# A fused linear-attention and feed-forward kernel: another form of the query feature map, an activation table taken early, one statistics pass moved

## The chip, the cores and the metric

The kernel runs on one core of a Trainium2 chip. The metric is the time of one execution on the device, in microseconds (us). A profile of one execution gives a span that is about 1.2 us shorter than the time of the same execution (209.1 of 210.31 for the kernel before). A run is called fast when it lies within 1.5% of the fastest run of its kernel; only fast runs are compared. All engines of the core are named as the profile names them: PE is the matmul engine (TensorE) and PEld its weight loads, DVE is VectorE, ACT is ScalarE, POOL is GpSimd, SP is the engine that issues most DMA transfers.

## The reference

One sequence of 2048 tokens of width 640 goes through a layer normalisation. Its result feeds a linear attention with 32 heads and a feed-forward block of width 1728, and the two are joined by a gate. Cut to what matters:

```python
xn = layernorm(x)
q, k, v = split(xn @ wqkv)                   # 32 heads of 20
phi = lambda t: where(t > 0, t + 1, exp(t)) + 1e-6
pq, pk = phi(q), phi(k)
kv  = einsum("bhsd,bhse->bhde", pk, v)
num = einsum("bhqd,bhde->bhqe", pq, kv)
den = einsum("bhqd,bhd->bhq", pq, sum_over_s(pk)) + 1e-6
s = (num / den) @ wo
u = relu(xn @ w1) @ w2
out = x + s * silu(u)
```

## The kernel before

The kernel works in this order: statistics, centring and transposes of the first four tiles of 128 tokens; keys; queries and `h = relu(xn w1)` by turns; the denominator of the attention; a Gram matrix of `xn` and the key features, from which `kv` follows; `kv` times `wo` as one fused weight; then `u` by 320-column products, the gates, and the output. Each `sc.op` puts one instruction on the named engine with the buffers that it reads (R) and writes (W).

The query feature map. A block of 128 features by 512 tokens stands in one of six PSUM banks; `er` holds three pairs of 16-bit buffers in SBUF:

```python
    def Q_block(j, f):
        b = nextb()                                   # a ring of 6 banks
        sc.group("PE", [... matmul(ps[b], lhsT=wq[:, k, ...], rhs=xnT[:, j, k, :]) for k in range(C)], ...)
        e_ = er[:, es, 0, :]
        r_ = er[:, es, 1, :]
        sc.op("ACT", lambda eng: eng.activation(out=e_, in_=ps[b], func=ACTF.Exp), ...)
        sc.op("DVE", lambda eng: eng.tensor_scalar(out=r_, in0=ps[b], scalar1=0.0, scalar2=1e-6,
                                                   op0=ALU.max, op1=ALU.add), ...)
        sc.op("DVE", lambda eng: eng.scalar_tensor_tensor(out=pqT[:, f, schunk(j)], in0=e_, scalar=1.0, in1=r_,
                                                          op0=ALU.min, op1=ALU.add), ...)
```

The head, where `bn` is the half-tile statistics pass (BATCH_NORM_STATS2) and `xcT_copy` takes transposed tiles out of PSUM:

```python
    K_mm(0, 2, 0, 1)
    transposes(1, 6)
    xcT_copy(0, 0, 1, "DVE")
    bn(0, 1)
    mean_act(2, 0)
    xcT_copy(1, 6, 0, "DVE")
    xcT_copy(1, 6, 1, "ACT")
    ...
    centre(2)
    transposes(2, 0)
```

The stretch where the fused weight meets the first gates. The reciprocal of the denominator goes through a scratch buffer in memory and comes back widened, in four parts, with which the query features are multiplied (`divide`):

```python
    load_recip(2)                        # DMA, issued by SP
    load_recip(3)
    fns = [...]                          # matmuls of the last Gram block
    lastG = sc.group("PE", fns, ...)
    sc.op("ACT", ... activation(out=GT[:, 4, :] ..., func=ACTF.Copy), ...)
    u_T(2); u_T(4)
    divide(1)
    ...
    def W_block(c, b):                   # one of six blocks of the fused weight
        sc.group("PE", ...)              # kv times wo: two matmuls
        # PSUM -> wtmp by VectorE (blocks 1 and 4) or ScalarE (the others), then row moves:
        dma("SP", lambda eng, q=q, e=e: eng.dma_start(wf[...], wtmp[...]), R=[("wtmp", c)], W=[("wf", q)])
    def gate_q(t, n, b):
        sc.op("ACT", lambda eng: eng.activation(out=g[:, HN*n:HN*(n+1)], in_=ps[b][:, 0:HN], func=ACTF.Silu), ...)
```

## Time and profile before

| | kernel before |
|---|---|
| time, median of 3 runs | 210.42 us (210.40 to 210.59) |
| profiled span | 209.1 us, granted PE clock 0.999 |
| busy: PE, VectorE, ScalarE, GpSimd | 204.3, 172.9, 109.1, 47.9 us |
| table load before the first gate | 1.28 us |
| PE standing before 138.65 us | 0.49 us |

The page of the kernel before: first the busy time of each engine with its share of the span and its instruction count, then the shares of the chain that ended last, then three of its groups (line, engine, operation, output and inputs, count; busy time and mean ns of one; idle time of the engine before them and what ended it).

```profile
PE 204.3 (98%) x1367; PEld 126.3 (60%) x1377; DVE 172.9 (83%) x321; ACT 109.1 (52%) x214; POOL 47.9 (23%) x71
...
PE 94%; ACT 2%; DVE 2%; DMA 1%; issue 0%
...
L580 DVE SCALAR_TENSOR_TENSOR pqT<-regE 128x512 bf16<-128x512 bf16 x20 | 17.0, 848 | 0.7
L578 DVE TENSOR_SCALAR regE<-psT 128x512 bf16<-128x512 f32 x20 | 13.6, 680 | 4.7 <-ACT regE L577 4.7
L577 ACT ACTIVATE regE<-psT 128x512 bf16<-128x512 f32 x20 | 11.9, 597 | 8.6 <-PE psT L570 8.1
```

The kernel is bound by PE. The two VectorE groups are the pair of passes that the change rewrites: 30.6 us of VectorE's 172.9, but their engine is not the one that ends last. There are 1377 weight loads and 1367 matmuls: ten matmul records are missing. Each missing record looks like a pause of 0.216 us between the starts of two PE instructions, and ten of the pauses that one could count in this trace are false.

The second pass has a wide spread. In the view of one line's instructions, the three figures after the colon are the shortest, median and longest in ns:

```profile
L580 DVE SCALAR_TENSOR_TENSOR pqT<-regE x20: 691/691/1816, 35.2 to 101.1; 128x512 bf16<-128x512 bf16 x20
```

The chain of waits in order of time (start, length, engine or cause), kernel before, its first part and the stretch before the first gate:

```profile
5.27 0.27 DVE regX L501
5.54 0.40 DVE stats L436
5.94 0.20 DVE regX L501
...
135.94 1.28 ACT L1043
137.22 0.01 issue
137.23 0.44 ACT wv_sb L1043
137.67 0.59 ACT reg L1017
138.26 0.34 ACT psT L806
138.60 0.05 issue
138.65 5.88 PE psT L799 x42
```

Most of the chain is PE itself. It leaves PE in the head, for a statistics pass that stands between two copies, and here, where ScalarE spends 1.28 us at L1043 with no operand. That is a table load for silu. The timeline of PE over the same stretch (start, length, then how many instructions; what the engine waited for stands in brackets) says what the load costs PE:

```profile
136.26 1.11 PE L799 MATMUL psT<-reg,regH 128*128 128x320 f16 x7
137.21 1.11 PE L799 MATMUL psT<-reg,regE 128*128 128x320 bf16 x7
138.65 0.58 PE L799 MATMUL psT<-reg,regH 128*128 128x320 f16 x3 [0.33 <-ACT psT L806]
```

Seven matmuls of 320 columns start 0.136 us apart: the group that began at 136.26 is followed by the next at 137.21, which is 0.95 us later. The group of 137.21 had thus given way at 138.16, and the next began at 138.65. PE lost 0.49 us of the 1.28 us that the load lasted; the queued matmuls covered the rest.

The timeline of VectorE, kernel before, at four places:

```profile
5.85 0.27 DVE L501 COPY regX<-psT 128x256 bf16<-128x256 bf16 x1
...
101.67 0.31 DVE L695 TENSOR_TENSOR zmat<-mh,psT 128x160 bf16<-128x160 f32 x1
...
130.43 1.56 DVE L737 TENSOR_TENSOR pqT<-pqT,reg 128x1024 bf16<-128x1024 bf16 x2 [1.24 <-DMA reg<-scr]
131.91 0.95 DVE L744 TENSOR_TENSOR reg<-psT,mv 128x360 bf16<-128x360 f32 x3
```

### The profile page before, as it was taken

What the parts mean: (1) busy time and instruction counts of PE and PEld (TensorE: products, weight loads), DVE (VectorE), ACT (ScalarE), POOL (GpSimd) and SP (SyncE); (2) the same over time, 40 slices, a digit from 0 to 9 for tenths busy, and PEclk for the clock granted to TensorE, in tenths of its full rate; (3) what the DMA queues carried; (4) which work ended last, traced back from release to release, by engine and by line L of the source; (5) the groups of instructions that cost most, each with busy time, mean ns of one, the idle gap of its engine ahead of it and who ended that gap; (6) DMA issues with size and microseconds to landing.
All of it is one profiled execution on the core that took longest, in us unless ns stands there. A gap on an engine that the chain in (4) does not pass through costs nothing.

```text
span 209.1 us, 3583 instructions
## 1 busy us (share of the span) xinstructions
PE 204.3 (98%) x1367; PEld 126.3 (60%) x1377; DVE 172.9 (83%) x321; ACT 109.1 (52%) x214; POOL 47.9 (23%) x71
## 2 busy tenths in 40 slices
PE   7999999999999999999999999999999999999995
PEld 7655554554554555444447777767777777777773
DVE  3988966798996899979997777888888989797465
ACT  5697766466665666655653432472435254343531
POOL 2278701111008389994000000000000000000001
PEclk9999999999999999999999999999999999999999
DMA  6988499122000217000189999337911010110103
GB/s 202 358 289 166 83 313 88 35 41 41 12 0 10 55 31 191 31 2 0 41 272 267 331 273 321 117 112 236 310 55 63 0 66 26 40 66 0 63 3 125
DMA packets 30359, 24.74 MB, mean 118 GB/s; under 512 B 12037, under 2 KB 30341, under 8 KB 30341
## 3 DMA queue, kind: packets, MB, share of 16 engines
q1 hardware_dynamic: 27013, 20.26, 35.0%
q10 hardware_dynamic: 3328, 4.24, 6.3%
q8 instruction: 11, 0.18, 0.4%
q14 instruction: 7, 0.06, 0.1%
HBM read 15.81 MB, written 5.24 MB: 101 GB/s over the span
## 4 chain that ended last, share of the span: by engine, by line
PE 94%; ACT 2%; DVE 2%; DMA 1%; issue 0%
PE psT L799 38%; PE psT L592 27%; PE psT L517 10%; PE psT L570 10%; PE psT L1218 3%; PE psT L1302 2%; DMA reg<-in_A_x_dram 1%; PE psT L611 1%; ACT reg L1017 1%; PE psT L983 1%; ACT L1043 1%; PE psT L704 1%; DVE stats L436 0%; PE psT L491 0%; PE psT L1009 0%
## 5 line engine op out<-in xcount | busy, mean ns | idle before, releaser
L592 PE MATMUL psT<-reg 128*128 128x512 bf16 x192 | 45.5, 379 | 0.3 <-issue 0.2
L596 ACT ACTIVATE regH<-psT 128x512 bf16<-128x512 f32 x52 | 30.8, 602 | 17.3 <-PE psT L592 17.3
L799 PE MATMUL psT<-reg,regH 128*128 128x320 bf16 (+1 forms) x224 | 34.4, 299 | 0.3 <-ACT psT L806 0.3
L592 PEld LDWEIGHTS psT<-reg 128*128 128x128 bf16 x195 | 18.9, 98 | 21.9 <-issue 0.4
L799 PEld LDWEIGHTS psT<-reg,regH 128*128 128x128 bf16 (+1 forms) x224 | 21.8, 98 | 9.1 <-ACT psT L806 0.7
L799 PE MATMUL psT<-reg 128*128 128x320 bf16 (+1 forms) x164 | 27.2, 299 | 0.0
L1211 POOL TENSOR_TENSOR reg<-reg 128x224 bf16<-128x224 bf16 x1 | 0.6, 605 | 109.5 <-DVE reg L1206 109.5
L528 POOL TENSOR_TENSOR wv_sb<-wv_sb,reg 128x640 f32<-128x640 f32 x16 | 24.0, 1501 | 1.9 <-DVE reg L552 1.0
L1043 ACT ACTIVATE wv_sb<-psT 128x320 bf16<-128x320 f32 x28 | 11.1, 437 | 25.2 <-PE psT L799 15.6
L744 DVE TENSOR_TENSOR psT<-psT,reg 128x320 f32<-128x320 f32 x30 | 14.3, 495 | 11.9 <-PE psT L799 11.1
L570 PE MATMUL psT<-reg 128*128 128x512 bf16 x95 | 23.8, 379 | 0.3
L534 ACT ACTIVATE regE<-psT 128x640 bf16<-128x640 f32 x24 | 15.6, 701 | 9.1 <-PE psT L517 9.1
L799 PEld LDWEIGHTS psT<-reg 128*128 128x128 f16 (+1 forms) x164 | 16.0, 98 | 6.4
L806 ACT ACTIVATE psT<-psT 128x320 f32<-128x320 f32 x32 | 13.7, 427 | 10.6 <-PE psT L799 10.0
L517 PE MATMUL psT<-reg 128*128 128x320 bf16 x120 | 18.3, 299 | 0.0
L580 DVE SCALAR_TENSOR_TENSOR pqT<-regE 128x512 bf16<-128x512 bf16 x20 | 17.0, 848 | 0.7
L578 DVE TENSOR_SCALAR regE<-psT 128x512 bf16<-128x512 f32 x20 | 13.6, 680 | 4.7 <-ACT regE L577 4.7
L570 PEld LDWEIGHTS psT<-reg 128*128 128x128 bf16 x100 | 9.8, 98 | 11.6
L806 ACT ACTIVATE reg<-psT 128x320 f32<-128x320 f32 (+1 forms) x22 | 9.6, 435 | 13.1 <-PE psT L799 13.1
L577 ACT ACTIVATE regE<-psT 128x512 bf16<-128x512 f32 x20 | 11.9, 597 | 8.6 <-PE psT L570 8.1
L436 DVE BATCH_NORM_STATS2 stats<-reg 128x6 f32<-128x320 bf16 x32 | 14.1, 474 | 2.3 <-DMA reg<-in_A_x_dram 2.3
L517 PEld LDWEIGHTS psT<-reg 128*128 128x128 bf16 x120 | 11.7, 98 | 6.5 <-DMA reg<-reg 0.2
(105 smaller groups left out, 305.2 us busy)
## 6 DMA issues: line engine op xcount, KB each, us to landing
scr<-rden SPq DMA_DIRECT2D x4, 640.0 KB, 10.0
reg<-in_A_x_dram SPq DMA_DIRECT2D x4, 640.0 KB, 6.1
out_dram<-reg SPq DMA_DIRECT2D x15, 160.0 KB, 1.9
reg<-in_A_x_dram SPq DMA_DIRECT2D x14, 160.0 KB, 3.4
reg<-scr SPq DMA_DIRECT2D x2, 640.0 KB, 7.4
regE<-scr SPq DMA_DIRECT2D x2, 640.0 KB, 7.2
reg<-in_B_w_dram ACTq DMA_DIRECT2D x1, 1040.0 KB, 7.1
reg<-in_A_wo_dram SPq DMA_DIRECT2D x6, 160.0 KB, 5.0
```

The lines of the kernel that those rows point to most:

```text
L436: sc.op("DVE", lambda eng: eng.bn_stats(stats[:, t, a, :], xv[:, HN * a:HN * (a + 1)]), R=[("xin", t % XR)], W=[("stats", t, a)])
L517: fns.append(lambda eng, a=a, k=k, lhs=lhs: eng.matmul(ps[b + a][:, 0:HN], lhsT=lhs, rhs=wk[:, k, HN * a:HN * (a + 1)], start=(k == 0), st ...
L528: sc.op("POOL", lambda eng: eng.tensor_tensor(out=zacc, in0=zacc, in1=pk[:, t, :], op=ALU.add), R=[("zacc",), ("pk", t)], W=[("zacc",)])
L534: sc.op("ACT", lambda eng: eng.activation(out=o_.rearrange("p (a n) -> p a n", a=2), in_=ps2(b, HN), func=func, scale=scale), R=[("ps", b) ...
L570: sc.group("PE", [(lambda eng, k=k: eng.matmul(ps[b], lhsT=wq[:, k, P * f:P * (f + 1)], rhs=xnT[:, j, k, :], start=(k == 0), stop=(k == C ...
L578: sc.op("DVE", lambda eng: eng.tensor_scalar(out=r_, in0=ps[b], scalar1=0.0, scalar2=1e-6, op0=ALU.max, op1=ALU.add), R=[("ps", b), ("er_e ...
L580: sc.op("DVE", lambda eng: eng.scalar_tensor_tensor(out=pqT[:, f, schunk(j)], in0=e_, scalar=1.0, in1=r_, op0=ALU.min, op1=ALU.add), R=[(" ...
L592: a = sc.group("PE", [(lambda eng, k=k: eng.matmul(ps[b], lhsT=w1_col(k, P * f, P), rhs=src[:, k, :], start=(k == 0), stop=(k == C - 1))) ...
L596: sc.op("ACT", lambda eng: eng.activation(out=hT[:, f, schunk(j)], in_=ps[b], func=ACTF.Relu), R=[("ps", b)], W=[("hT", j, f)])
L744: sc.op("DVE", lambda eng: eng.tensor_tensor(out=out, in0=in0, in1=in1, op=op), R=R, W=W, extra=extra)
L799: sc.group("PE", [(lambda eng, k=k, lhs=lhs, rhs=rhs: eng.matmul(ps[b][:, 0:HN], lhsT=lhs, rhs=rhs, start=(start and k == 0), stop=(k == n ...
L806: sc.op("ACT", lambda eng: eng.activation(out=dst, in_=ps[b][:, 0:HN], func=ACTF.Copy), R=[("ps", b)], W=[dkey], extra=extra)
```

## The change

It has three parts. First, the query feature map is written as max(x + 1, min(exp x, 1)). For x > 0 the first term is the larger, since x + 1 > 1; for x ≤ 0 the second is, since exp x ≥ x + 1. So one pass clips the exponential in place, in SBUF and in 16 bit, and a second pass reads PSUM and takes the maximum; the pass with two SBUF inputs is gone. Second, a one-column silu is put before the last Gram block, so that the table load falls into ScalarE's idle time there. Third, the statistics of tile 0's second half move behind the copy that they stood before.

```diff
@@ -573,13 +573,12 @@
         es = qi[0] % NER
         qi[0] += 1
         e_ = er[:, es, 0, :]
-        r_ = er[:, es, 1, :]
         sc.op("ACT", lambda eng: eng.activation(out=e_, in_=ps[b], func=ACTF.Exp), R=[("ps", b)], W=[("er_e", es)])
-        sc.op("DVE", lambda eng: eng.tensor_scalar(out=r_, in0=ps[b], scalar1=0.0, scalar2=1e-6, op0=ALU.max, op1=ALU.add),
-              R=[("ps", b), ("er_e", es)], W=[("er_r", es)])
-        sc.op("DVE", lambda eng: eng.scalar_tensor_tensor(out=pqT[:, f, schunk(j)], in0=e_, scalar=1.0, in1=r_,
-                                                          op0=ALU.min, op1=ALU.add),
-              R=[("er_e", es), ("er_r", es)], W=[("pqT", j, f)])
+        sc.op("DVE", lambda eng: eng.tensor_scalar(out=e_, in0=e_, scalar1=1.0, scalar2=1e-6, op0=ALU.min, op1=ALU.add),
+              R=[("er_e", es)], W=[("er_e", es)])
+        sc.op("DVE", lambda eng: eng.scalar_tensor_tensor(out=pqT[:, f, schunk(j)], in0=ps[b], scalar=1.0 + 1e-6,
+                                                          in1=e_, op0=ALU.add, op1=ALU.max),
+              R=[("ps", b), ("er_e", es)], W=[("pqT", j, f)])
 
     def hsrc(j):
         if j == 0:
@@ -633,9 +632,9 @@
     K_mm(0, 2, 0, 1)
     transposes(1, 6)
     xcT_copy(0, 0, 1, "DVE")
-    bn(0, 1)
     mean_act(2, 0)
     xcT_copy(1, 6, 0, "DVE")
+    bn(0, 1)
     xcT_copy(1, 6, 1, "ACT")
     K_mm(0, 2, 1, KA)
     K_mm(1, 4, 0, KA)
@@ -1302,6 +1301,8 @@
             fns.append(lambda eng, t=t, a=a: eng.matmul(
                 ps[4 + a][:, 0:HN], lhsT=xn[:, t, P * 4:P * 5], rhs=pk[:, t, HN * a:HN * (a + 1)],
                 start=(t == 0), stop=(t == T - 1)))
+    sc.op("ACT", lambda eng: eng.activation(out=msum[:, 3, 0:1], in_=zero[:, 0:1], func=ACTF.Silu),
+          R=[("zero",)], W=[("msum", 3, 0)])
     lastG = sc.group("PE", fns, R=[("xn", t) for t in range(T)] + lo8 + hi8, W=[("ps", 4), ("ps", 5)])
     sc.op("ACT", lambda eng: eng.activation(out=GT[:, 4, :].rearrange("p (a n) -> p a n", a=2), in_=ps2(4, HN),
                                             func=ACTF.Copy),
```

Between the first part and the third, lines stand one number lower in the changed kernel than before; after the third, one number higher.

## The prediction

> **What bounds the kernel.** TensorE: the page gives PE 98% busy, VectorE 83%, ScalarE 52%; the chain of waits is 94% PE at a granted clock of 0.999. In the timeline, matmuls start 0.216 us apart (512 columns) and 0.136 us apart (320) nearly everywhere. PE is held up in three places: the head (to about 8.8 us), a few hundredths at 97–104 us, and a gap before 138.65 us, where fused-weight blocks meet the first gates.
>
> **1. Query feature map.** Each of 20 blocks has an exponential (ScalarE, 0.60 us) and two VectorE passes. Before: max/add from PSUM (mean 0.68 us, 13.6 in all), then min/add with two SBUF inputs (0.69 us undisturbed, mean 0.85, worst 1.82 beside GpSimd's sums; 17.0 in all). After: an in-place 16-bit tensor_scalar in SBUF, then one pass over PSUM. The Trainium skill (VectorE: DVE Perf Modes, perf-mode tier table) gives the first the 4x mode; the trace agrees: the key map's 128x640 pass takes 0.27–0.32 us undisturbed, but 1.52 beside GpSimd. I estimate 0.28 us (1.2–1.5 in the four or so blocks beside GpSimd) and 0.69 us for the PSUM pass everywhere. The pair falls from 30.6 to about 23.5 us, VectorE busy from 172.9 to about 166.
> On the critical path: almost nothing. In the query stage PE runs back to back; 18 of 20 exponentials wait for PE. A PSUM bank is now released by the second pass, about 0.3 us later, but the six-bank ring returns only after some 6 us. A smaller VectorE backlog at 99–102 us may give 0.05–0.15 us before the denominator.
>
> **2. Silu table.** The load (1.28 us) stands at 135.94 us in the chain. It moves into ScalarE's 3.91 us idle time during the last Gram block, so it becomes free. (The skill's ScalarE: Activation LUTs, "What ACT_TABLE_LOAD costs", adds a 1.38 us drain; here the next activation begins 0.01 us after the load.) But PE doesn't lose 1.28 us: from 137.21 it had seven matmuls of 0.136 us, so it could have gone on at 138.16 and did at 138.65. Without the load the PSUM copy waits for its own matmuls and ends near 137.8. Gain 0.49 us.
>
> **3. Sums of tile 0.** One 0.48 us pass stands between two copies of transposed tiles; the chain charges it 0.40 us. The second copy then waits for its transposes (issued 5.33, copy 0.32 us later by tile 0's example), so it starts at 5.65, not 5.85. Tile 2's centring still waits for its mean (6.40), its transposes until 6.88, so about 0.1 us survives.
>
> **Sum:** 0.5 + 0.1 + 0.1 = 0.7 us. Predicted 209.7 us, 8 in 10 between 209.1 and 210.2. Faster by over 2%: 1%; within 2%: 97.5%; slower: 1.5%.
>
> **What would show it.** First query pass near 0.28 us, second near 0.69; VectorE busy down 6–8 us; the query stage's length unchanged; the table load at about 125 us, in a gap, and none later; PE's wait before the first gates (0.33 us in the wait table) gone; the first long run of 512-column matmuls 0.1 us earlier than 11.98; the chain still about 95% PE.
>
> **What would make it wrong.** The in-place pass beside GpSimd waits so long that the bank ring stalls PE (slower by up to 1 us); a PSUM pass much slower than 0.69 us; another table load later; tile loads landing at other times in the head, swallowing the 0.1 us; a second wait just behind the removed one at 138 us; or gaps on PE that modelled matmul ends hide, making the gain 1–1.5 us.

## The result

| | before | after |
|---|---|---|
| time, median of 6 runs | 210.50 us (210.33 to 211.21) | 210.06 us (209.79 to 210.66) |
| profiled span | 209.1 us | 208.9 us |
| busy: PE, VectorE | 204.3, 172.9 us | 205.2, 160.3 us |
| the two VectorE passes of the query map | 30.6 us | 21.5 us |
| PE standing before the first gates' products | 0.49 us | 0 |

All of these runs were fast. A ratio here is the mean time of one kernel's fast runs over the mean of the other's in the same rounds, so it is not quite the ratio of the medians. For after over before it is 0.9975, with a 95% interval of 0.9954 to 0.9996: about 0.5 us gained, with 0.1 to 1.0 us inside the interval. PE's busy time rose mostly because all its 1377 records are there this time: e3_sums below, with the query map of before and all records, shows 204.9 us.

The page of the changed kernel (the last line is the same group with shapes kept apart):

```profile
PE 205.2 (98%) x1377; PEld 126.6 (61%) x1377; DVE 160.3 (77%) x321; ACT 109.7 (53%) x215; POOL 45.8 (22%) x71
...
PE 97%; DMA 1%; DVE 1%; issue 0%
...
L577 DVE TENSOR_SCALAR regE<-regE 128x512 bf16<-128x512 bf16 x20 | 7.7, 386 | 9.6 <-ACT regE L576 9.5
...
L579 DVE SCALAR_TENSOR_TENSOR pqT<-psT,regE 128x512 bf16<-128x512 f32 x20 | 13.8, 692 | 0.7
```

The two lines' instructions, shortest, median and longest:

```profile
L577 DVE TENSOR_SCALAR regE<-regE x20: 239/287/1517, 34.4 to 98.2; 128x512 bf16<-128x512 bf16 x20
L579 DVE SCALAR_TENSOR_TENSOR pqT<-psT,regE x20: 691/692/693, 34.8 to 98.5; 128x512 bf16<-128x512 f32 x20
```

The pass over PSUM takes the same time in all twenty blocks. The spread went into the in-place pass, whose median is 0.287 us and whose worst is 1.517 us.

The table load, in the timeline of ScalarE of the changed kernel:

```profile
125.10 0.44 ACT L805 ACTIVATE reg<-psT 128x320 bf16<-128x320 f32 x1 [0.65 <-PE psT L798]
125.56 1.28 ACT L1304 ACT_TABLE_LOAD   x1
126.85 0.20 ACT L1304 ACTIVATE msum<-zero 128x1 f32<-128x1 bf16 x1
129.45 0.70 ACT L1307 ACTIVATE reg<-psT 128x640 bf16<-128x640 f32 x1 [2.39 <-PE psT L1301]
```

The load ends at 126.84 us, and ScalarE is idle for another 2.39 us after it. There is no later load. PE at the place of the old gap, timeline of the changed kernel:

```profile
136.55 1.11 PE L798 MATMUL psT<-reg,regH 128*128 128x320 f16 x7
137.50 1.11 PE L798 MATMUL psT<-reg,regE 128*128 128x320 bf16 x7
138.46 0.84 PE L798 MATMUL psT<-reg,regH 128*128 128x320 f16 x5
```

The steps are now 0.95 and 0.96 us: PE doesn't stop. But the stretch begins 0.29 us later than before (136.55 against 136.26). The weight loads of PE and the timeline of VectorE of the changed kernel show where that was lost:

```profile
132.79 0.11 PEld L1008 LDWEIGHTS psT<-reg 128*128 128x128 bf16 x2 [0.35 <-DVE reg L743]
133.21 0.11 PEld L1008 LDWEIGHTS psT<-reg 128*128 128x128 bf16 x2 [0.31 <-DVE reg L743]
```

```profile
5.84 0.29 DVE L501 COPY regX<-psT 128x256 bf16<-128x256 bf16 x1 [0.27 <-PE psT L491]
...
99.11 0.31 DVE L694 TENSOR_TENSOR zmat<-mh,psT 128x160 bf16<-128x160 f32 x1
...
130.73 1.56 DVE L736 TENSOR_TENSOR pqT<-pqT,reg 128x1024 bf16<-128x1024 bf16 x2 [2.26 <-DMA reg<-scr]
132.21 0.95 DVE L743 TENSOR_TENSOR reg<-psT,mv 128x360 bf16<-128x360 f32 x3
```

VectorE stood 2.26 us (1.24 before) for the second part of the reciprocal, so its division began at 130.73 instead of 130.43, and the evacuation of `kv` behind it at 132.21 instead of 131.91. The load of that part had been issued earlier than before (122.91 against 123.64 us) but took 7.80 us to land instead of 6.78. The fused-weight matmuls need that evacuation and waited twice; the pauses between PE's matmuls are 0.19 and 0.14 us. The gain of 0.49 us at the gates was thus partly given back 5 us earlier in the same stretch.

Since the head of the kernel varies from run to run, the experiments compare two parts of each profile: the head, up to the first weight load of a 512-column product of `w1`, and the body, the span minus the head. Before: head 11.63, body 197.43. After: head 11.63, body 197.23.

### The profile page after: what moved, and what is told of

It reads as the page before. It is cut to its first block, busy times and chain, and to the rows that moved or that the text cites. A ratio compares the mean times of both kernels' runs of the same rounds, so it can differ in the third digit from the quotient of the medians.

```text
span 208.9 us, 3582 instructions
## 1 busy us (share of the span) xinstructions
PE 205.2 (98%) x1377; PEld 126.6 (61%) x1377; DVE 160.3 (77%) x321; ACT 109.7 (53%) x215; POOL 45.8 (22%) x71
## 4 chain that ended last, share of the span: by engine, by line
PE 97%; DMA 1%; DVE 1%; issue 0%
PE psT L798 40%; PE psT L591 27%; PE psT L517 11%; PE psT L570 10%; PE psT L1217 3%; PE psT L1301 2%; DMA reg<-in_A_x_dram 1%; PE psT L610 1%; PE psT L1008 1%; PE psT L491 1%; PE psT L982 1%; PE psT L703 1%; DVE stats L436 0%; DVE reg L1205 0%; DVE reg L1210 0%; DVE reg L484 0%
## 5 line engine op out<-in xcount | busy, mean ns | idle before, releaser
L591 PE MATMUL psT<-reg 128*128 128x512 bf16 x195 | 46.0, 379 | 0.0
L570 PE MATMUL psT<-reg 128*128 128x512 bf16 x100 | 24.8, 379 | 0.0
L528 POOL TENSOR_TENSOR wv_sb<-wv_sb,reg 128x640 f32<-128x640 f32 x16 | 23.1, 1442 | 1.9 <-DVE reg L552 1.0
L577 DVE TENSOR_SCALAR regE<-regE 128x512 bf16<-128x512 bf16 x20 | 7.7, 386 | 9.6 <-ACT regE L576 9.5
L591 PE MATMUL psT<-regX,reg 128*128 128x512 bf16 x65 | 14.8, 379 | 0.0
```

The source lines that it names most:

```text
L528: sc.op("POOL", lambda eng: eng.tensor_tensor(out=zacc, in0=zacc, in1=pk[:, t, :], op=ALU.add), R=[("zacc",), ("pk", t)], W=[("zacc",)])
L570: sc.group("PE", [(lambda eng, k=k: eng.matmul(ps[b], lhsT=wq[:, k, P * f:P * (f + 1)], rhs=xnT[:, j, k, :], start=(k == 0), stop=(k == C ...
L591: a = sc.group("PE", [(lambda eng, k=k: eng.matmul(ps[b], lhsT=w1_col(k, P * f, P), rhs=src[:, k, :], start=(k == 0), stop=(k == C - 1))) ...
```

## The experiments

The theory was that the table load is the whole gain in the body, that the query rewrite is off the critical path, and that moving the sums is worth 0.1 us in the head. The first rival was that the shorter VectorE queue carries the gain. A second question came from the changed profile: is the wait at 133 us a cost of the change, or chance? Each of the first three experiments does one part of the change alone on the kernel before.

### e1_table: the silu alone

```diff
+    sc.op("ACT", lambda eng: eng.activation(out=msum[:, 3, 0:1], in_=zero[:, 0:1], func=ACTF.Silu), ...)
     lastG = sc.group("PE", fns, ...)
```

> The kernel before with the early silu table alone. Theory 1 (only the table load sat on TensorE's path, and only 0.49 us of its 1.28 us): 0.3 to 0.7 us faster than before, ratio 0.997 to 0.9985; TensorE's gap of 0.49 us before the first gates (at about 138.6 us) gone, VectorE busy unchanged near 173 us. Theory 2 (the gain comes from VectorE's 12.6 us less work): within 0.15 us of before, ratio 0.9993 or more. Theory 3 (the whole load was on the path): 1.3 us faster, ratio 0.994.

The five fast runs had a median of 210.42 us against 210.76 us for before, ratio 0.9979 (0.9961 to 0.9997). The profiled execution was a slow one of 440.29 us, so its trace can't be compared. PE in that execution, timeline:

```profile
199.54 2.61 PE L592 MATMUL psT<-reg 128*128 128x512 bf16 x5
201.87 2.61 PE L570 MATMUL psT<-reg 128*128 128x512 bf16 x5
```

Five matmuls took 2.33 us from one group to the next, 0.466 us each instead of 0.216. The whole execution ran at about half pace. The timing supports the theory; the place of the gain had to be looked up in e1b_table.

### e2_query: the query rewrite alone

The diff is the first hunk of the change.

> The kernel before with the new query feature map alone. Theory 1: within 0.2 us of before, or up to 0.3 us slower if the second division's load again lands late (VectorE then evacuates the fused weights' input behind it); VectorE busy near 160 us; the 0.49 us gap before the first gates still there. Theory 2: 0.4 to 0.6 us faster, ratio 0.997 to 0.998.

The median was 210.76 us against 210.76, ratio 1.0001 (0.9981 to 1.0021). VectorE's busy time fell to 160.3 us, all of the reduction that the whole change shows, and the body was 197.38 us, 0.05 less than before. The pause of 0.49 us before the gates was still there, as PE's timeline in this experiment shows:

```profile
138.94 0.31 PE L798 MATMUL psT<-reg,regH 128*128 128x320 f16 x1 [0.33 <-ACT psT L805]
```

A rewrite that frees 12.6 us of VectorE is worth nothing that these runs can see. The interval of the ratio alone would still allow a gain of 0.4 us; together with the body and the pause it rules out that the rewrite carries the gain.

### e3_sums: the moved statistics alone

The diff is the second hunk of the change.

> The kernel before with the sums of tile 0 moved back, alone. Theory 1: within 0.15 us of before, since tile 2's centring waits for its own mean; the fourth group of key matmuls starts at 6.2 us if the first part of the key weight lands late and at about 6.0 us if it lands early, and the transposes of tile 2 start at 6.9 to 7.0 us in any case. Rival: the 0.40 us that the chain charges is all gained, ratio 0.998.

The median was 210.45 us against 210.76, ratio 0.9986 (0.9970 to 1.0002). The copy behind the moved pass, timeline of VectorE in this experiment:

```profile
5.71 0.29 DVE L501 COPY regX<-psT 128x256 bf16<-128x256 bf16 x1 [0.15 <-PE psT L491]
```

It began at 5.71 instead of 5.85 us, and the head was 11.50 instead of 11.63: 0.13 us. The body was 197.41, as before. In the changed kernel's own profile the same copy began at 5.84, since it waited for its transposes, and the head was 11.63. So the step seems to be worth about 0.13 us at most (one profile of each, and the head scatters by more than that from run to run), and it disappears when the head's data arrive later.

This trace has all 1377 matmul records and settles another point. The pause on PE right behind the denominator's matmuls is 0.095 us, with the old query map. The changed kernel's is 0.095 us too. In the trace of before the same pause reads 0.323 us; without one false 0.216 it is 0.107. In front of the denominator's matmuls, which are the ones that need `zmat`, no pause shows: they began at 102.04 us before and at 102.02 after, with PE's preceding group starting at the same times in both profiles.

### e4_hold: the changed kernel, with two reciprocal loads held back

The second part of the reciprocal shares the DMA queues with the third and the fourth. Here these two are issued only after the second has landed.

```diff
-    load_recip(2)
-    load_recip(3)
     fns = []
 ...
     lastG = sc.group("PE", fns, ...)
     sc.op("ACT", ... activation(out=GT[:, 4, :] ..., func=ACTF.Copy), ...)
+    load_recip(2, [recip_at[1]])         # waits for the DMA of part 1
+    load_recip(3)
```

> The changed kernel, with the loads of reciprocals 2 and 3 held back until reciprocal 1 has landed. Theory: in the changed kernel these loads compete with reciprocal 1, VectorE waits 2.26 us for it before the second division, and the evacuation for the fused weights, behind it in VectorE's order, costs TensorE two gaps of 0.19 and 0.14 us at 132.8 us. With the loads held, reciprocal 1 lands 1 to 3 us sooner, the division starts before 130 us, the two gaps vanish, and the time is 0.3 us below the changed kernel's: ratio to before 0.9955 to 0.9970. Rival: the landing is set by the stores and the value weight's load in front of it, nothing changes: ratio 0.9975.

The division in the timeline of VectorE:

```profile
129.75 1.56 DVE L738 TENSOR_TENSOR pqT<-pqT,reg 128x1024 bf16<-128x1024 bf16 x2 [1.00 <-DMA reg<-scr]
131.66 1.16 DVE L745 TENSOR_TENSOR reg<-psT,mv 128x360 bf16<-128x360 f32 x3 [0.34 <-PE psT L984]
```

The wait fell from 2.26 to 1.00 us, the pauses at 133 us were gone, and the evacuation of `kv` now waits for PE and no longer for a DMA. The body was 196.88 us, 0.35 less than the changed kernel's. The time was 210.08 us, ratio 0.9973 (0.9953 to 0.9993), no better than the changed kernel and above the 0.9955 to 0.9970 expected. This profile's head was 12.08 us: PE reached its full pace only at about 6.3 us there. So e4 shows the gain in one body and not in the time, where the rival's 0.9975 fits as well.

### after_again and e1b_table: second looks at the changed kernel and at the table alone

> The changed kernel once more, for a second look and as the neighbour of the split kernel on one chip. Theory: from the first weight load for the 512-column matmuls to the end (the body) it takes 196.9 to 197.3 us, where the kernel before takes 197.43; which of the two ends depends on whether the second division (VectorE, waiting for a reciprocal) starts before or after about 130.4 us. The head before that scatters between 11.5 and 12.1 us with the moment when TensorE reaches full speed and with the landing of the first key weight. Ratio to before 0.9965 to 0.998. Rival: the two gaps at 132.8 us come with the change every time (a body of 197.2 again, the same two gaps), because the earlier first division shifts the reciprocal's load.

> The early table alone, again, since its one profile fell into a run of 439 us in which TensorE's matmuls ran at half speed from start to end. Theory 1: body 196.9 to 197.0 us (0.48 less than before), no gap at 138.6 us, table load at about 125 us; ratio 0.997 to 0.999. Theory 3 (whole load on the path): body 196.1.

The changed kernel took 210.35 us against 210.62, ratio 0.9985 (0.9970 to 1.0001), and its body was 197.20 us. There was no pause at 133 us this time, but one of 0.31 us at 144.34. VectorE and PE's weight loads in after_again:

```profile
143.79 1.95 DVE L743 TENSOR_TENSOR reg<-reg 128x640 f16<-128x640 bf16 x4 [0.96 <-DMA reg<-reg]
```

```profile
144.34 1.20 PEld L1217 LDWEIGHTS psT<-reg,pqT 128*128 128x128 bf16 x10 [0.48 <-DVE reg L743]
```

VectorE waited for the last of the ten row moves of the fused weight, which SP issues one after the other; that series took 8.26 us to issue, against 7.62 us in the first profile of the changed kernel and 7.83 us in the kernel before. The expectation had tied the body to the second division: started before 130.4 us, it should have been near 196.9 us. The division started at 130.27 and the body was still 197.20, so that part failed. Both profiles of the changed kernel lose about 0.3 us after the removed wait or just before it, but at two different places.

The table alone took 210.23 us, ratio 0.9982 (0.9966 to 0.9998), and its body was 196.91 us, 0.52 less than before, with neither of these pauses. PE at the gates in e1b_table, timeline:

```profile
137.40 1.11 PE L799 MATMUL psT<-reg,regE 128*128 128x320 bf16 x7
138.35 0.84 PE L799 MATMUL psT<-reg,regH 128*128 128x320 f16 x5
```

The step is 0.95 us, seven matmuls without a stop. The predicted size of the table step was 0.49. Here it is measured in the body, in the one place where the pause disappeared.

### e5_swap: the opposite, two table loads before the first gate

One gelu on one column is put just before the first gate, in the kernel before. It forces a load for gelu and a second load for silu.

```diff
     def gate_q(t, n, b):
+        if first gate:
+            sc.op("ACT", lambda eng: eng.activation(out=msum[:, 3, 0:1], in_=zero[:, 0:1], func=ACTF.Gelu), ...)
         g, sl = g_of(t)
```

> The kernel before with one more table load (a Gelu of one element per partition) just ahead of the first gate, so that two loads stand where one stood. Theory 1 (the first 0.8 us of delay at that place is hidden behind queued matmuls, everything more is paid in full): 1.4 to 1.5 us slower than before (1.28 for the load, 0.15 to 0.2 for the activation), the gap before the first gates 1.9 to 2.0 us instead of 0.49. Rival (a load there costs TensorE a fixed 0.49 us each): 0.5 to 0.6 us slower.

ScalarE and PE in this experiment:

```profile
136.60 1.28 ACT L1045 ACT_TABLE_LOAD   x1
137.90 0.20 ACT L1045 ACTIVATE msum<-zero 128x1 f32<-128x1 bf16 x1
138.12 1.28 ACT L1048 ACT_TABLE_LOAD   x1
```

```profile
140.83 1.40 PE L799 MATMUL psT<-reg,regH 128*128 128x320 f16 x9 [1.84 <-ACT psT L806]
```

The time was 212.29 us, ratio 1.0088 (1.0059 to 1.0118), the body was 198.93 us, 1.50 more than before, and the pause grew from 0.49 to 2.01 us. The extra load with its small activation takes 1.28 + 0.20 us and a few hundredths of issue on ScalarE, and PE stands for all of it. The first load costs PE 0.49 us and the second 1.5: only the first finds queued matmuls to hide behind.

### e8_split and e8b_split: e4 with the first key weights in two transfers

```diff
-    wk_load(0, 2)
+    wk_load(0, 1)
+    wk_load(1, 2)
```

> The changed kernel with the reciprocal loads held and with the first key-weight load split in two, so that the first key matmul waits for 160 KB, not 320 KB. Theory: the body stays at 196.9 us; the first key matmul starts at 5.0 to 5.1 us in every profile rather than at 5.0 to 5.6, the head is 0 to 0.3 us shorter; ratio to before 0.9955 to 0.9970. It would fail if the extra issue on the SyncE queue (0.43 us) delays tiles 3 to 5 or the later weights more than that.

> The kernel with held reciprocal loads and split key-weight load again, as the neighbour of the next: body 196.8 to 196.95 us, ratio 0.9955 to 0.9975.

The times were 209.87 us, ratio 0.9965 (0.9947 to 0.9983), and 210.13 us, ratio 0.9968 (0.9953 to 0.9984). Both bodies were 196.85 us. The split itself didn't do what it was made for: the first key matmul's weight load came at 5.12 us in one profile and at 5.35 in the other, where 5.0 to 5.1 was expected, and the heads were 11.54 and 11.77 us. What these kernels share with e4 is the held loads; the head is left to chance. That the hold brings the second part of the reciprocal forward is not certain either: in e8b_split VectorE still waited 1.79 us for it, and the division began at 130.23 us, as late as in e1b_table (130.21) without the hold.

### e6_before_extra and e7_after_extra: is VectorE's slack real?

If the query map is off the critical path, more of it should cost little. In e6 the pass over PSUM of the kernel before is issued twice; in e7 the changed kernel gets one more such pass, whose result nobody reads, between its two passes.

```diff
+        sc.op("DVE", lambda eng: eng.tensor_scalar(out=r_, in0=ps[b], scalar1=0.0, scalar2=1e-6, op0=ALU.max, op1=ALU.add), ...)
         sc.op("DVE", lambda eng: eng.scalar_tensor_tensor(...), ...)
```

> The kernel before with its first query pass (max and add from PSUM, 0.68 us) issued twice in each of the 20 blocks: about 13 us more VectorE work, busy near 186 us. Theory: before the denominator VectorE has no slack in this kernel (the block-diagonal z matrix is made at 101.67 us and TensorE asks for it at about 101.8), and the backlog of the last query blocks adds up, so TensorE stalls there: 2 to 4 us slower, with one gap before the denominator matmuls holding most of it. Rival (VectorE is off the critical path, so its work is free): within 0.3 us of before.

> The changed kernel with the same PSUM pass added in each query block, its result unused: VectorE busy near 173 us, as in the kernel before. Theory: the query change bought VectorE about 2.6 us of slack before the denominator (the z matrix at 99.11 us instead of 101.67) and no time; spending it costs 0 to 0.6 us against the changed kernel, ratio to before 0.997 to 1.001. Rival (the gain of the change comes from VectorE's relief): the kernel falls back to before's time or beyond, ratio 1.000 to 1.010, with new gaps on TensorE through the query stage because banks are held longer.

Both expectations were too small, and e7's ratio fell into the range that its rival had named (1.000 to 1.010). It doesn't revive that rival, since e2_query, the rewrite alone, gained nothing and kept the pause. e6 took 220.77 us, ratio 1.0480 (1.0462 to 1.0498), body 207.68: 10.25 us for 12.5 us more of VectorE's busy time (185.4). e7 took 211.78 us, ratio 1.0051 (1.0034 to 1.0069), body 198.62: 1.4 us more than the changed kernel for 13.5 us more (173.8). Timeline of PE in e6:

```profile
55.15 1.25 PE L570 MATMUL psT<-reg 128*128 128x512 bf16 x5 [0.93 <-DVE regE L581]
...
75.41 1.66 PE L517 MATMUL psT<-reg 128*128 128x320 bf16 x10 [2.61 <-DMA reg<-reg]
76.86 2.34 PE L570 MATMUL psT<-reg 128*128 128x512 bf16 x5
...
112.43 1.26 PE L707 MATMUL psT<-pqT,zmat 128*32 128x512 bf16 x20 [1.27 <-DVE zmat L698]
```

Three different waits opened: for a PSUM bank that VectorE had not released (55.15), for a transposing DMA whose normalisation stood behind the query passes in VectorE's queue (75.41), and for `zmat`, the operand of the denominator (112.43). After the pause of 2.8 us at 75 us PE also ran for about 3.4 us at half pace: the five matmuls in 2.34 us show it, and the trace has a granted clock of 0.5 from 76.7 to 80.1 us. That stretch alone holds about 1.5 us of the 10.25. e7 shows the second kind, 1.18 us at 70.56 us, and a wait of 0.43 us at 101.51 us for a query pass to release a PSUM bank.

So slack has two sides. The kernel before had just enough of it: more work of 12.5 us costs 10 us, while 12.6 us less work gains nothing. With the change the extra pass costs 1.4 us instead of 10.25. The reading that fits is that the rewrite moved the kernel away from an edge that it had been standing near, and the time didn't change because it hadn't been over it. The total of VectorE's busy time doesn't tell where that edge is: e7 has about as much (173.8 us) as the kernel before (172.9) and has two waits that the kernel before hasn't.

### e9_queues: e8 with half of the row moves issued by GpSimd

```diff
-            dma("SP", lambda eng, q=q, e=e: eng.dma_start(wf[...], wtmp[...]), ...)
+            dma(("SP", "POOL")[len(wkeys) % 2], lambda eng, q=q, e=e: eng.dma_start(wf[...], wtmp[...]), ...)
```

> As the split kernel, with every second of the ten moves of fused-weight rows issued from GpSimd's queue rather than all ten from SyncE's, where their issue takes 7.6 us in a row. Theory: in the changed kernel's second profile VectorE waited 0.96 us for the last of these moves and TensorE lost 0.31 us at 144.3 us; that wait stands 0.3 us or less behind the removed one. With two queues the last move lands 1 to 2 us sooner, and the gap at 144 us can't return; the body stays at 196.8 to 196.9 us, since in the split kernel's profile that gap was already absent. Ratio equal to the split kernel's within 0.0010. It would be worse if moves issued by GpSimd take longer to issue or land than on SyncE's queue, or slow VectorE.

SP's five moves now went out between 134.76 and 138.81 us, and the loads behind them began at 138.86 us. The body was 196.85 us, as in e8. The time was 209.94 us (5 runs), ratio 0.9962 (0.9948 to 0.9976). That can't be told from e8_split. The issuing of the row moves is not what limits a kernel in which the loads are held.

Together, e8 and e9 beat the kernel before by about 0.35%, in three groups of runs. Against the changed kernel there is only one comparison on the same chip, the means of e8_split and after_again, 209.90 and 210.37 us, 0.2% apart; no interval was taken of it, each group spreads over about 0.9 us, and e8_split's profile also had the shorter head. So it is not shown that they beat the changed kernel.

## Why the prediction was right or wrong

**The time.** Predicted were 209.7 us, 209.1 to 210.2, and a change within 2%. Measured were 210.06 us (210.35 in the second look, a little above the range) with ratios of 0.9975 and 0.9985. The direction, the class and the mechanism were right; the gain was 0.3 to 0.5 us where 0.7 had been predicted. The intervals of the ratios (0.1 to 1.0 us, and 0 to 0.6 us) are too wide to tell these apart; what was mis-sized is read from the bodies and heads below.

**The silu table: right in place and size.** "Gain 0.49 us" was read from seven matmuls of 0.136 us that were still queued. The table alone shortened the body by 0.52 us and removed exactly that pause (e1b_table). Doubling the load added 1.50 us in the same place (e5_swap). The load now lies at 125.56 us, where "about 125 us" was written. The Trainium skill (ScalarE: Activation LUTs, "What ACT_TABLE_LOAD costs") adds a drain of some 1.38 us to a load of about 1.28; the load agrees, but in the changed kernel it began within 0.02 us of the end of the activation in front of it, and the next one began 0.01 us after it (126.85). The same page ("Table sets: the hidden batching unit") says that cheap functions such as copy are in every set; this is borne out here, as the Copy at 129.45 us came after the silu load and no further load followed. That is what makes an early load safe.

**The query map: right about the path, too low about VectorE.** "On the critical path: almost nothing" holds: ratio 1.0001 alone, body 0.05 us shorter. The pass times were 0.287 us by median and 0.692, for which 0.28 and 0.69 had been written. Two steps failed. "VectorE busy down 6–8 us" was 12.6: the pair saved 9.1 (30.6 to 21.5), since one in-place pass of twenty took over 1 us where four had been estimated, and 3.5 us more came from VectorE passes that the change doesn't touch, above all the in-place pass of the key map, from 9.9 to 6.8 us in all. The Trainium skill (SBUF — State Buffer, "SBUF: two separate sides") describes one port pair that VectorE and GpSimd can't both hold, taken by VectorE's two-port fast modes and by passes with two SBUF inputs. The traces fit this: the two-input pass reached 1.816 us and the in-place pass 1.517, each beside GpSimd work, while the pass over PSUM with a single SBUF input took 0.691 to 0.693 us in all twenty blocks, though eight of them overlapped GpSimd work by more than 0.5 us. That the key passes became shorter for this reason was not tested by itself.

**"0.05–0.15 us before the denominator": wrong, it is 0.** `zmat` was made 2.56 us earlier (99.11 instead of 101.67), but PE began the denominator's matmuls only 0.02 us earlier. The step that failed is the VectorE backlog: it ended just in time for PE in the kernel before, so clearing it freed nothing. The one pause that shows nearby, right behind the denominator, was mostly a missing record: complete traces of both query forms show 0.095 us.

**"About 0.1 us survives" in the head: right in one profile, absent in the other.** e3_sums showed 0.13 us. In the changed kernel's profile the first key weights landed later (first key weight load at 5.22 us against 5.03), and the head was as long as before. "Tile loads landing at other times in the head, swallowing the 0.1 us" was among the things that would make the prediction wrong, and this is what happened. Over all profiles the head ran from 11.50 to 12.31 us. It follows the arrival of the first key weights (5.03 to 5.57) and the moment when PE's small matmuls change from 107 to 56 ns, at about 3.7 us in the profile of before and as late as 6.7 us in e5_swap. The three longest heads (12.08 to 12.31 us) are those in which the change came at 6.3 to 6.7 us; e2_query's 11.97 has the latest weights (5.57). The Trainium skill (TensorE: Matmul & The Clock Gate, Part 1) says that the array starts at half rate and changes after a busy window that is not tied to the kernel's start, so that the moment varies; it names 0.5 us to either side, and the profiles here show more.

**What was missing from the sum: about 0.3 us given back.** This is the main mis-sized term. The text named "a second wait just behind the removed one at 138 us" as a risk and put nothing in the sum for it. It came, once at 133 us (a division that waited for its DMA) and once at 144 us (the last row move). The bodies say it in one line: table alone 196.91, whole change 197.23 and 197.20, whole change with held loads 196.88 and three times 196.85 us.

**What stays open.** The pauses were there in both profiles of the whole change, in none of the four with held loads, and not in the one usable profile of the table alone. Does the query rewrite bring the loss about? The other profiles speak against it. e2_query has the rewrite and no pause at 133 us. Counted from the end of the head, the load of the second part was issued after 111.1 us in e1b_table and e3_sums, with the old map, and in e2_query and after_again, with the new one (111.3 in the first profile of the changed kernel, 112.0 before). What differs is the time that the load takes to land: 7.80 us in the changed kernel's first profile, the longest of all, 6.8 to 7.6 us in the others without the hold, 6.5 to 7.3 us with it. The issue of the ten row moves scatters in the same way, from 7.6 to 8.3 us; it took 8.15 us in e3_sums and 8.25 us in e5_swap, where PE had stood at the gates and so came later to the place that needs them; no pause showed there. This points to chance in the DMAs, some of which the removed wait had covered, and not to a cost of the rewrite. It is not shown: two profiles of the whole change and one of the table alone are too few. Whether holding the loads helps, or the four profiles with held loads were lucky, is open too, and why it should help the late row move is not known.

## What to carry to other kernels

The cost of a table load, or of any stop on a helper engine, is the part that the bound engine's queued work doesn't cover: 0.49 us of 1.28 for the first load here, and all of 1.5 for a second one. Relieving an engine that nobody waits for gained nothing that could be measured here (12.6 us of VectorE's time), yet that says nothing about how much more it can bear: adding the same amount to the kernel before cost 10 us. After a wait is removed, look at the next few microseconds of DMA and of the engines behind it, and count the records of a trace before believing its small gaps.

## What the Trainium skill lacked or had wrong

- ScalarE: Activation LUTs, "What ACT_TABLE_LOAD costs": the drain of about 1.38 us that it adds to a load was not there. In the kernel before, the changed kernel and e5_swap the next activation began 0.01 to 0.02 us after the load, in the kernel before and the changed kernel the load began within 0.02 us of the end of the one in front, and removing a load from the path gained 0.52 us.
- VectorE: DVE Perf Modes, "The perf-mode tier table": scalar_tensor_tensor is not in the table. Undisturbed, a 128x512 pass took 0.691 us with two 16-bit SBUF inputs and 0.692 us with one of them in PSUM at 32 bit, so 16 bit gave it no gain that shows, while tensor_scalar in SBUF took 0.287 us.
- TensorE: Matmul & The Clock Gate, Part 1: the change to full pace fell between about 3.7 and 6.7 us in profiles of nearly equal kernels, a wider spread than the 0.5 us to either side that is stated. One execution ran at about half pace from end to end (440.29 us, 0.466 us for a 512-column matmul) while its granted clock read 1.0. The page warns that the trace's clock events can be unreliable and that the gate has been seen stuck, but at another ratio and for some 50 us; a whole execution at half pace isn't described.
